# A fused retention and expert-attention kernel: another order of matmuls within a step

## The chip, the cores and the metric

One core of a Trainium2 chip runs the kernel. The metric is the device time of one execution in microseconds (us), which is the time of that one core. The kernel before was timed in three runs.

## The reference

Two layers stand one behind the other. The first is a retention layer without softmax: for 8 batches, 8 heads, 576 positions and a head dimension of 64, the scores are weighted with a power of gamma that depends on the distance, and masked causally.

```python
gamma = 1.0 - 2.0 ** (-5.0 - np.arange(H))
Dmat = np.where(rel >= 0, gamma[:, None, None] ** rel, 0.0)    # rel = i - j
attn = np.matmul(q @ k.T / 8 * Dmat, v)
x = attn.transpose(0, 2, 1, 3).reshape(B, S, H * D)            # 8 x 576 x 512
```

The second layer takes x, picks 2 of 4 experts for each position with a small gate, and runs a causal softmax attention with one head of 64 in each expert. The outputs of the two chosen experts are added with the weights of the gate.

```python
logits = x @ w_gate                  # top 2 of 4, softmax over these two: w
for e in range(4):
    q, k, v = x @ wq[e], x @ wk[e], x @ wv[e]
    a = softmax(causal(q @ k.T / 8))
    out += chosen(e) * w(e) * (a @ v @ wo[e])
```

All inputs and outputs are float32.

## The kernel before, in words

**Steps.** The retention is computed in the chunked form, with chunks of 64 positions and a running state per head. A step n takes 128 positions (two chunks) of two batches, so 36 steps (NC) cover everything; nine steps make one pair of batches. In the retention of a step there are four kinds of small float32 matmuls, all 64 by 64 on a quarter of the TensorE array:

- `qk(n)` (L115 to L132): the products of queries and keys inside a chunk. ScalarE copies them from PSUM to `p` (L127) and GpSimd masks them (L130).
- the *old* products in `result` (L155): state times query. ScalarE copies them to `x32` (L158).
- the *own* products in `result` (L168): values times the masked products of the same chunk. VectorE adds them to `x32` (L172 copies where there is no state yet, L173 adds).
- `state(n)` (L106): the new state's products `st`, which VectorE adds to the state (L111 copies for a first chunk, L113 adds).

`result(n)` is a generator; each `yield` is a place where the caller puts other work between. Its later parts scale `x32` with powers of gamma on GpSimd (L178) and split it into a high part `xh` (ScalarE, L181) and a low part `xl` (GpSimd, L183), so that the big projections can run as three float32r products each.

**The second layer's work.** `proj` (L213) makes keys or queries of two experts for 384 positions with twelve 128 by 384 matmuls (L226) in three groups of four, with a yield behind each group. `vproj` (L241) makes values and gate logits (L251). `outproj` (L431) is the last product (L440). `scores` and `score` (L322 to L380) do the softmax attention's scores of a tile of 128 positions: the first `next` issues all of the tile's score matmuls `ss` (L354, or L360 for the last, 64 wide tile of a batch), and the rest is the softmax, where VectorE masks, takes the row's extreme and moves the scores out of PSUM (L369, L373), and ScalarE does the exponential (L377). One step later `factors` (L382) and `scale` (L391) scale the rows, and `turn` (L398) transposes them by VectorE into the buffers `TA` and `TB` (L403, L405). When all of a batch's tiles are turned, `values` (L408) multiplies them with the values: 18 column blocks of the scores, for each 8 float32 matmuls (L418) into four PSUM tiles `ys`, which are accumulated over all blocks; then ScalarE and VectorE take them out as `yh` and `yl` (L424, L425).

**The order of the work.** Every engine is listed in `ORDERED`, so each engine executes its instructions in the order in which the program text issues them. The main loop (L677 on) does for each step n from 4 to 36: `factors` of the last step's tiles, `qk(n)`, the first part of `result(n-1)` (old, then own), `state(n)`, then, from step 7 (LAG) on, the score matmuls of this step's tiles, the scaling and the softmax, the loads for step n+2, the rest of `result`, and `work(n)`. A table, `STEPS`, written out by hand, says which projections, value products and output products step n does; `work(n)` issues them in the order keys and queries, values' projection, value products, output products, and between its pieces the loop issues transposes. In the steps with value products (12, 17, 22, 26, 31 and 35; `hold` in the code) the transposes come after all of `work`, because they would overwrite `TA` and `TB`. Behind the value products' place in `work` stands a count: before the change they are issued, all at once, when three groups of projections have been issued, which is after the keys and before the queries. Step 12 has only value products.

**PSUM.** All matmul results use one pool of eight banks (`pool`, `bufs=8`): `qk`, `old`, `own` and `st` take two banks each, a projection or an output product one, `ys` four. A step's scores take four banks, but two where the tile is one of the first two of a batch and stands alone (steps 7, 8, 16, 17, 25, 26, 34 and 35). A bank is given again in the order in which it is released, and TensorE waits in its queue when the tile that had the bank before has not been read out.

Of the kernel before, what the change touches and what calls it, by code (L numbers as in the profile page):

```python
# [27 lines left out]
LAG = 7  # L28


def f(ap):
    return ap.bitcast(F32)
# [3 lines left out]
def kernel(ctx: ExitStack, tc: tile.TileContext, xf, vkf, wraw,  # L36
# [14 lines left out]
    def bank(shape, name):  # L51
        return pool.tile(shape, F32, name=name, tag="b")
# [34 lines left out]
    def subs(n):  # L87
        return [divmod(2 * n + s, 9) for s in range(2)]
# [49 lines left out]
    def result(n):  # L138
        if n % 3 == 0:
            XR[n // 3] = [sa.tile([128, 4, NB], F32R, name="x" + y, bufs=2) for y in "hl"]  # L140
        xh, xl = XR[n // 3]
        l0 = n % 3 * 128
        old = [bank([128, 2, 128], "old") for g in range(2)]
        x, p, vk = X[n], P.pop(n), VK[n]
        x32 = sa.tile([128, 2, 2, 128], F32, name="x32", tag="x32", bufs=2)
        on, off = slice(0, 128), None
        for s, (b, k) in enumerate(subs(n)):
            i = slice(64 * s, 64 * s + 64)
            if k == 0:
                on, off = slice(64 - 64 * s, 128 - 64 * s), i  # L150
                continue
            for r in range(2):
                for g in range(2):
                    for u in range(2):
                        mm(old[g][HALF[u], r, i], S_[b, k - 1][HALF[g], r, u], x[HALF[g], 0, 2 * r + u, i],  # L155
                           start=True, stop=True)
        for g in range(2):
            act(x32[:, g, :, on], old[g][:, :, on], AF.Copy)  # L158
        if n == 4:
            build(4)  # L160
            gp.tensor_copy(gi[:, :, S:], gi[:, :, :64])
        own = [bank([128, 2, 128], "own") for r in range(2)]
        for s in range(2):
            i = slice(64 * s, 64 * s + 64)
            for g in range(2):
                for r in range(2):
                    for u in range(2):
                        mm(own[r][HALF[u], g, i], vk[HALF[r], s, 0, 2 * g + u], p[HALF[r], g, s, u],  # L168
                           start=True, stop=True)
        for r in range(2):  # L170
            if off:
                v.tensor_copy(x32[:, :, r, off], own[r][:, :, off])  # L172
            v.tensor_add(x32[:, :, r, on], x32[:, :, r, on], own[r][:, :, on])  # L173
        x32 = x32.rearrange("p g r i -> p (g r) i")
        yield
        e = gp if n > 2 else v
        t0 = 64 * subs(n)[0][1]
        e.tensor_mul(x32, x32, gi[:, :, t0:t0 + 128])  # L178
        if n > 4:
            decay(n + 2)  # L180
        act(xh[:, :, l0:l0 + 128], x32, AF.Copy)  # L181
        yield
        e.tensor_sub(xl[:, :, l0:l0 + 128], x32, f(xh[:, :, l0:l0 + 128]))  # L183
        yield
# [220 lines left out]
                v.transpose(TB[:, :nb - 8, z, k - 4], x[:, 8:])  # L405
            yield

    def values(b, s0, s1, cut=True):  # L408
        py = [bank([128, s1 - s0, 32], "ys") for g in range(4)]
        order = [j for m in range(s1) for j in (m, 2 * s1 - 1 - m)]  # L410
        for m, j in enumerate(order):
            sj = max(s0, j // 2)
            R, i = divmod(18 * b + j, 12)
            vq, jj = VQ[R], i % 4 * 3 + i // 4
            for z in range(2):
                tt = TA[:, j, z, sj:s1] if j < 8 else TB[:, j - 8, z, sj - 4:s1 - 4]
                for g in range(4):
                    mm(py[g][HALF[z], sj - s0:], vq[QUAD[g], jj, D * z:D * z + D], tt[QUAD[g]],  # L418
                       start=(m == 0), stop=(m == 2 * s1 - 1))
            if cut and m % 6 == 5 and m < 2 * s1 - 1:  # L420
                yield
        for g in range(4):
            hi, lo = (y[:, g // 2, 1 + s0:1 + s1, g % 2] for y in YS)
            act(hi, py[g], AF.Copy)  # L424
            v.tensor_sub(lo, py[g], f(hi))  # L425
        if b % 2 == 0:
            for y in YS:
                gp.tensor_copy(y[:, :, 0], f(y[:, :, 9]))
        yield
# [26 lines left out]
    STEPS = {}  # L456
    for P_ in range(NP):
        b, n = 2 * P_, 9 * P_
# [28 lines left out]

    def work(n):
        todo = STEPS.get(n, [])
        vals = [values(x[1], 0, 9, False) for x in todo if x[0] == "y"]  # L490
        bring = [x[1] for x in todo if x[0] == "back"]
        i = 0
        for kind, *w in todo:
            if kind == "kq":
                R, p, *m = w
                for m in m or "kq":
                    for _ in proj(R, m, p):
                        i += 1
                        for y in vals[:i == 3]:
                            next(y, None)  # L500
                        if i == 3 and bring:
                            back(bring.pop())
                        yield
            elif kind == "v":
                for _ in vproj(*w):
                    i += 1
                    if i == 3 and bring:
                        back(bring.pop())
                    yield
            elif kind == "o":  # L510
                for y in vals:
                    next(y, None)
                yield from outproj(w[0])
        for y in vals:
            for _ in y:
                yield
        for R in bring:
            back(R)

    def run(g):  # L520
        for _ in g:
            pass
# [114 lines left out]

    late = result(0)
    next(late)
    qk(1)  # L640
    fetch("k", nc.scalar)
    fetch("q", nc.scalar)
# [4 lines left out]

    late = result(1)
    next(late)
    qk(2)  # L650
    next(late)
    run(late)
    state(2)

    late = result(2)
    next(late)
    load(3, nc.scalar)
    weights("k", "h")
# [18 lines left out]
    for n in range(4, NC + 1):  # L677
        if n < LAG:
            load(n + 2)
        if n == 5:  # L680
            fetch("o")
        late = result(n - 1)
        now, old = TILES.get(n, []), TILES.get(n - 1, [])
        for x in old:
            factors(*x)
        if n < NC:
            qk(n)
        next(late)
        if n < NC:
            state(n)  # L690
        if n >= LAG:
            soft = scores(*now)
            next(soft)
            run(each(scale, old))
            run(soft)
            load(n + 2)
        gates(0)
        if n <= 5:
            decay(n + 1)
        run(late)  # L700
        for w in {4: "v", 7: "o"}.get(n, ""):
            weights(w)
        turns = each(turn, old)
        if n == 12:
            run(turns)
        hold = any(w[0] == "y" for w in STEPS.get(n, []))
        for _ in work(n):
            if not hold:
                next(turns, None)
        run(turns)  # L710
        if n < NC:
            gates(1)
# [53 lines left out]
```

## Time and profile before

| | us |
|---|---|
| median of three runs | 428.38 |
| lowest and highest | 424.47 and 432.3 |
| the profiled execution | 426.58 |
| its span, first to last instruction | 424.7 |
| TensorE matmul busy | 393.2 |
| VectorE busy | 265.3 |
| ScalarE busy | 283.4 |
| GpSimd busy | 167.3 |

The span is what the views below divide up; 1.9 us of the execution lie outside it. A float32 matmul of the program is two matmul and two weight-load instructions in the trace. Matmul ends are modelled, so that a short stall can hide inside time shown as busy; the starts are recorded. In the text a step is named by its number n; step 19 starts at 169.75 us, step 20 at 179.03, step 21 at 189.38, step 22 at 199.12, step 24 at 222.80, step 26 at 243.08, step 30 at 286.64 and step 31 at 295.59, each time being that of its first `qk` matmul.

### The profile page before, as it was taken

How to read it: one execution, taken by the hardware profiler on the slowest of the kernel's cores; microseconds unless marked ns; L12 is line 12 of the kernel's file. 1: busy time of each engine (PE TensorE's matmuls, PEld its weight loads, DVE VectorE, ACT ScalarE, POOL GpSimd, SP SyncE). 2: the span in 40 equal slices, each digit the busy share in tenths (PEclk: the TensorE clock that was granted, in tenths of full speed). 3: DMA queues.
4: the chain of work that ended last, by engine and by line, in shares of the span. 5: the costliest groups of instructions: out<-in, count | busy, mean ns of one | idle time of the engine just before them, and what ended most of it. 6: DMA issues, size and time to landing. Idle time of an engine off the chain costs nothing.

```text
span 424.7 us, 20358 instructions
## 1 busy us (share of the span) xinstructions
PE 393.2 (93%) x8742; PEld 333.8 (79%) x8742; DVE 265.3 (62%) x1103; ACT 283.4 (67%) x809; POOL 167.3 (39%) x182
## 2 busy tenths in 40 slices
PE   7597999996799999999998989999999999999894
PEld 3486898796688978897887978898788987887673
DVE  2745386765777726869296727677497726983931
ACT  4354469674597747878576747779587747797751
POOL 2217856443345534445354444444445432000000
PEclk9898999998999999999999999999999999999999
DMA  8568557464255536567264635566454221422331
GB/s 288 164 235 323 172 187 184 131 185 131 102 168 159 191 101 174 165 176 243 98 166 135 188 127 158 183 174 199 145 169 146 86 75 42 115 66 96 105 119 60
DMA packets 33689, 65.10 MB, mean 153 GB/s; under 512 B 3392, under 2 KB 19264, under 8 KB 33600
## 3 DMA queue, kind: packets, MB, share of 16 engines
q1 hardware_dynamic: 32304, 59.08, 44.4%
q10 hardware_dynamic: 1296, 4.72, 3.2%
q8 instruction: 69, 1.13, 1.2%
q14 instruction: 20, 0.16, 0.2%
HBM read 49.63 MB, written 14.16 MB: 150 GB/s over the span
## 4 chain that ended last, share of the span: by engine, by line
PE 83%; DVE 6%; issue 5%; DMA 3%; ACT 1%; SPq 1%; ACTq 1%; DVEq 0%
PE pj L226 25%; PE pv L251 13%; PE ys L418 12%; PE po L440 10%; PE ss L354 7%; PE qk L124 4%; PE own L168 4%; DMA vk<-vkf 3%; PE old L155 3%; PE st L106 3%; PE ss L360 2%; DVE yl L425 1%; DVE x L173 1%; DVE ta L403 1%; DVE p L369 1%
## 5 line engine op out<-in xcount | busy, mean ns | idle before, releaser
L377 ACT ACTIVATE p<-p,nm 128x64 f32<-128x64 f32 (+5 forms) x144 | 79.3, 552 | 18.0 <-DVE nm L369 13.4
L130 POOL TENSOR_SCALAR_AFFINE_SELECT p<-p 64x512 f32<-64x512 f32 x72 | 49.0, 680 | 95.4 <-ACT p L127 93.0
L395 ACT ACTIVATE p<-p,sm 128x64 f32<-128x64 f32 (+5 forms) x144 | 69.4, 567 | 9.5 <-DVE sm L389 5.6
L183 POOL TENSOR_TENSOR xl<-x,xh 128x512 fp32r<-128x512 f32 x33 | 42.4, 1284 | 60.5 <-ACT xh L181 60.5
L369 DVE CUSTOM_DVE_ANT_0 p<-ss,mask 128x128 f32<-128x128 f32 (+7 forms) x128 | 50.4, 452 | 4.4 <-PE ss L354 4.3
L173 DVE TENSOR_TENSOR x<-x,own 128x256 f32<-128x256 f32 (+1 forms) x72 | 25.5, 386 | 43.0 <-ACT x L158 35.7
L425 DVE TENSOR_TENSOR yl<-ys,yh 128x288 fp32r<-128x288 f32 (+2 forms) x36 | 12.8, 417 | 61.6 <-ACT yh L424 61.6
L178 POOL TENSOR_TENSOR x<-x,gi 128x512 f32<-128x512 f32 x33 | 42.5, 1289 | 18.2 <-DVE x L173 11.3
L403 DVE STREAM_TRANSPOSE ta<-p 128x256 f32<-128x256 f32 (+2 forms) x144 | 48.9, 367 | 0.2 <-ACT p L395 0.2
L418 PE MATMUL ys<-ta,vq 32*64 32x288 f32 (+6 forms) x1152 | 45.4, 365 | 3.8 <-issue 3.8
L418 PE MATMUL ys<-tb,vq 32*64 32x96 f32 (+4 forms) x1344 | 43.5, 248 | 5.0 <-issue 5.0
L418 PEld LDWEIGHTS ys<-tb,vq 32*64 32x64 f32 x1344 | 39.3, 134 | 7.2 <-issue 6.3
L418 PEld LDWEIGHTS ys<-ta,vq 32*64 32x64 f32 x1152 | 36.0, 133 | 8.4 <-issue 7.2
L354 PE MATMUL ss<-k,q 64*64 64x512 f32 (+7 forms) x512 | 38.5, 406 | 0.2 <-issue 0.2
L424 ACT ACTIVATE yh<-ys 128x288 fp32r<-128x288 f32 (+2 forms) x36 | 10.9, 389 | 38.1 <-PE ys L418 38.1
L448 ACT ACTIVATE ot<-po 128x512 f32<-128x512 f32 x35 | 19.9, 592 | 19.8 <-PE po L440 16.2
L95 POOL TENSOR_TENSOR vk<-vk,con 128x512 f32<-128x512 f32 x30 | 31.5, 1051 | 0.0
L127 ACT ACTIVATE p<-qk 128x256 f32<-128x256 f32 x72 | 23.7, 382 | 9.3 <-PE qk L124 8.3
L181 ACT ACTIVATE xh<-x 128x512 fp32r<-128x512 f32 x36 | 22.3, 618 | 10.5 <-POOL x L178 8.6
L106 PE MATMUL st<-vk 64*64 64x64 f32 x1024 | 24.1, 220 | 5.6 <-DVE vk L95 4.0
L113 DVE TENSOR_TENSOR s<-st,s 128x128 f32<-128x128 f32 x112 | 24.9, 281 | 6.2 <-PE st L106 6.2
L168 PE MATMUL own<-p,vk 64*64 64x64 f32 x1152 | 26.4, 222 | 2.0 <-issue 1.9
(86 smaller groups left out, 892.0 us busy)
## 6 DMA issues: line engine op xcount, KB each, us to landing
x<-xf SPq DMA_DIRECT2D x33, 512.0 KB, 4.5
vk<-vkf SPq DMA_DIRECT2D x33, 512.0 KB, 5.7
vq<-hv SPq DMA_DIRECT2D x48, 192.0 KB, 6.3
out<-ot SPq DMA_DIRECT2D x36, 256.0 KB, 2.3
hv<-vn SPq DMA_DIRECT2D x24, 192.0 KB, 2.6
ta<-wraw ACTq DMA_DIRECT2D x3, 512.0 KB, 5.6
x<-xf ACTq DMA_DIRECT2D x3, 512.0 KB, 4.3
vk<-vkf ACTq DMA_DIRECT2D x3, 512.0 KB, 6.2
```

Of the source, the lines that this page charges most:

```text
L130: gp.affine_select(w, w, pattern=[[0, 8], [1, 64]], base=0, channel_multiplier=-1, compare_op=OP.is_ge, fill=0.0)
L168: mm(own[r][HALF[u], g, i], vk[HALF[r], s, 0, 2 * g + u], p[HALF[r], g, s, u], start=True, stop=True)
L178: e.tensor_mul(x32, x32, gi[:, :, t0:t0 + 128])
L226: mm(ps, ww[:, kc, p * 128:(p + 1) * 128], xx[:, kc], start=(i == 0), stop=(i == 11))
L251: mm(ps, xx[:, kc, l0:l0 + 128], ww[:, kc], start=(i == 0), stop=(i == 11))
L354: mm(ps[u][HALF[p]], q(p, z, i), k[p][HALF[z], :ws[u]], start=True, stop=True)
L369: v.tensor_tensor_reduce(x, ps[u], mask[:, 512 - ws[u]:], -1.0, BIG, OP.add, OP.min, nm[:, u:u + 1])
L377: act(x, x, AF.Exp, bias=bias, scale=-1.0, accum_out=sm[:, 0, u:u + 1])
L395: act(x, x, AF.Copy, scale=sm[:, 1, u:u + 1])
L403: v.transpose(TA[:, :min(nb, 8), z, k], x[:, :min(nb, 8)])
L418: mm(py[g][HALF[z], sj - s0:], vq[QUAD[g], jj, D * z:D * z + D], tt[QUAD[g]], start=(m == 0), stop=(m == 2 * s1 - 1))
L440: mm(ps, yy[:, p], ww[:, p], start=(i == 0), stop=(i == 5))
```

## The change

Two things are moved; no instruction is added or taken out.

In the steps without value products, the score matmuls of step n are issued between the old and the own products. In the steps with value products they stay behind `state(n)`. For that, `result` has one more yield, between old and own, and the three calls ahead of the loop that want both parts call `next` twice.

In the steps with value products, `values` is cut in two halves of nine column blocks. The first half is issued first in `work(n)`, ahead of the projection of the keys; the second half when four groups of projections have been issued, which is after the keys and the first third of the queries. The tail's calls of `values` keep their cut of six blocks.

```diff
@@ result
             gp.tensor_copy(gi[:, :, S:], gi[:, :, :64])
+        yield
         own = [bank([128, 2, 128], "own") for r in range(2)]
@@ values
-    def values(b, s0, s1, cut=True):
+    def values(b, s0, s1, part=6):
...
-            if cut and m % 6 == 5 and m < 2 * s1 - 1:
+            if m % part == part - 1 and m < 2 * s1 - 1:
                 yield
@@ work
-        vals = [values(x[1], 0, 9, False) for x in todo if x[0] == "y"]
+        vals = [values(x[1], 0, 9, 9) for x in todo if x[0] == "y"]
...
+        for y in vals:
+            next(y)
...
-                        for y in vals[:i == 3]:
+                        for y in vals[:i == 4]:
                             next(y, None)
@@ the main loop
         next(late)
+        hold = any(w[0] == "y" for w in STEPS.get(n, []))
+        if n >= LAG:
+            soft = scores(*now)
+        if n >= LAG and not hold:
+            next(soft)
+        next(late)
         if n < NC:
             state(n)
         if n >= LAG:
-            soft = scores(*now)
-            next(soft)
+            if hold:
+                next(soft)
             run(each(scale, old))
             run(soft)
             load(n + 2)
```

The line that computed `hold` further down is gone. VectorE's and ScalarE's own orders in a step without value products stay as they were: adds of own, adds of the state, softmax.

More of the change, by code (lines that the diff above doesn't have):

```diff
@@ L649 @@
     next(late)
+    next(late)
     qk(2)
@@ L655 @@
     late = result(2)
+    next(late)
     next(late)
@@ L688 @@
         next(late)
+        hold = any(w[0] == "y" for w in STEPS.get(n, []))
[3 more added lines that the diff above has]
+            next(soft)
+        next(late)
         if n < NC:
@@ L705 @@
             run(turns)
-        hold = any(w[0] == "y" for w in STEPS.get(n, []))
         for _ in work(n):
```

## The prediction

> **What bounds the kernel now.** I read the page first, then the waits, then the timelines of single steps.
>
> ```profile
> span 424.7 us, 20358 instructions
> PE 393.2 (93%) x8742; PEld 333.8 (79%) x8742; DVE 265.3 (62%) x1103; ACT 283.4 (67%) x809; POOL 167.3 (39%) x182
> PE 83%; DVE 6%; issue 5%; DMA 3%; ACT 1%; SPq 1%; ACTq 1%; DVEq 0%
> q8 instruction: 69, 1.13, 1.2%
> ```
>
> TensorE is busy for 93% of the span, and the chain that ended last is TensorE for 83%. A busy share is no proof, so next come the waits of TensorE alone, in the stretch from 60 to 350 us, which is nearly all of the main loop:
>
> ```profile
> PE ys L418 <- issue: 7.0, 5, 3.8
> PE pj L226 <- DVE x L173: 2.0, 2, 1.4
> PE st L106 <- issue: 1.5, 1, 1.5
> PE ss L360 <- issue: 1.1, 1, 1.1
> PE old L155 <- issue: 1.0, 1, 1.0
> ```
>
> That is all but 0.2: 12.8 us of 290. Every other phase follows the one before without a gap. So whatever the order of the matmuls, the change can give back at most these 12.8 us, and of them 3.8 stand ahead of the value products of step 12, which wait for transposes and keep their place, and 1.4 in step 13 come from VectorE. About 7.5 us are within reach. On the other side nothing protects TensorE: each new wait of it is paid in full. The question is therefore which new waits the new order makes.
>
> **How a projection waits for VectorE.** Step 31 shows it.
>
> ```profile
> 297.28 1.40 PE L354 MATMUL ss<-k,q 64*64 64x320 f32 x15
> 298.76 0.16 DVE L389 TENSOR_TENSOR sm<-sm,wt 128x4 f32<-128x4 f32 x1
> 298.87 0.75 DVE L173 TENSOR_TENSOR x<-x,own 128x256 f32<-128x256 f32 x2
> 299.54 0.48 DVE L111 COPY s<-st 128x128 f32<-128x128 f32 x2
> 299.34 0.97 PE L226 MATMUL pj<-xh,whk 128*128 128x384 f32 x4 [0.66 <-DVE x L173]
> ```
>
> A step with four score banks uses eight banks for qk, old and the scores, and four for own and st; the first tile of `work` gets the bank that is released next, the first of own. VectorE was late here (L389 is the last step's factors), its add began at 298.87, and the projection started 0.47 after that start. In all but two steps this wait is hidden, because the state products and the scores run on TensorE while VectorE adds:
>
> ```profile
> 170.50 0.66 PE L168 MATMUL own<-p,vk 64*64 64x64 f32 x32
> 170.97 0.66 PE L106 MATMUL st<-vk 64*64 64x64 f32 x32
> 171.25 0.29 DVE L172 COPY x<-own 128x128 f32<-128x128 f32 x1 [3.65 <-PE own L168]
> 171.43 1.81 PE L354 MATMUL ss<-k,q 64*64 64x448 f32 x16
> 171.51 0.29 DVE L173 TENSOR_TENSOR x<-x,own 128x128 f32<-128x128 f32 x1
> 173.17 0.62 PE L226 MATMUL pj<-xh,whk 128*128 128x384 f32 x2
> ```
>
> In step 19 VectorE begins on own 0.28 after st begins; the first bank is free at about 171.80, and the projection starts at 173.17. The cover is the scores.
>
> **Part 1, the scores between old and own.** Now own and st are last, so only st's 0.46 (170.97 to 171.43) is left as cover. VectorE begins 0.28 after st begins, as the row shows, and the projection can start 0.47 later (step 31): 0.28 + 0.47 - 0.46 = 0.3 us of new wait. In steps 10, 14, 19, 23, 28 and 32 a batch begins and VectorE does a copy and an add for the first bank (171.25 to 171.80, 0.55, and 0.1 for the release): 0.28 + 0.65 - 0.46 = 0.47. Steps 7, 8, 16, 25, 34 have two score banks and use old's banks next, 36 has no st and qk: nothing. Step 13 waits for a late VectorE already. That leaves, without 21 and 30 (below), nine steps at 0.3 and six at 0.47: 2.7 + 2.8 = 5.5 us. In two of them (10 and 24) a stall of another kind falls behind own and hides 0.8: **+4.7**. Bounds: 0, if the adds are done within st's time, and 0.9 a step (VectorE's whole add and release, 0.75 + 0.1), 13 us.
>
> What else moves with it: own and st are some 1.2 to 1.7 us later. VectorE already stood idle ahead of own; it waits for ScalarE's copy of old as it is:
>
> ```profile
> DVE x L173 <- ACT x L158: 35.7, 18, 4.0
> vk<-vkf SPq DMA_DIRECT2D x33, 512.0 KB, 5.7
> ```
>
> Its chain through the step starts up to 1.75 later (step 19: 173.17 - 0.46 + 0.28 = 172.99, against 171.25). The load of `vk` waits in SyncE's queue for own, with hv, vq and out behind it, so all go out 1.2 to 1.7 later; vk lands 5.7 after its issue and is wanted by GpSimd a step (9 us) later, so this costs nothing here. If that cover were gone it would cost up to the 1.7 in a step.
>
> **Part 2, values first.** Four `ys` banks are wanted at once where one projection bank was. In steps 17, 26 and 35 (two score banks) they are old's two and own's two:
>
> ```profile
> 244.77 0.97 PE L354 MATMUL ss<-k,q 64*64 64x192 f32 x15
> 245.11 0.76 DVE L173 TENSOR_TENSOR x<-x,own 128x256 f32<-128x256 f32 x2 [1.48 <-ACT x L158]
> 245.67 0.96 PE L226 MATMUL pj<-xh,whk 128*128 128x384 f32 x4
> ```
>
> Both adds end at 245.87 and the fourth bank is free at 245.96, where TensorE wants it at 245.67: 0.3 each, and 0.3 more in step 17, whose VectorE comes later: **+1.2**. In steps 22 and 31 they are own's two and st's two, so L111 too must be done, and VectorE is late from the step before:
>
> ```profile
> 191.41 0.75 DVE L173 TENSOR_TENSOR x<-x,own 128x256 f32<-128x256 f32 x2 [3.48 <-ACT x L158]
> 201.17 0.74 DVE L173 TENSOR_TENSOR x<-x,own 128x256 f32<-128x256 f32 x2
> 201.83 0.48 DVE L111 COPY s<-st 128x128 f32<-128x128 f32 x2
> 202.15 0.97 PE L226 MATMUL pj<-xh,whk 128*128 128x384 f32 x4
> 288.67 0.75 DVE L173 TENSOR_TENSOR x<-x,own 128x256 f32<-128x256 f32 x2 [3.48 <-ACT x L158]
> 289.80 0.72 PE L440 MATMUL po<-who,yh 128*128 128x512 f32 x2
> ```
>
> Between the adds at 191.41 and at 201.17 VectorE has no rest, as between 288.67 and 298.87. In step 30 st would begin 0.46 ahead of the output products at 289.80 and the add 0.28 behind that, at 289.62: 0.95 later than now, and with it all that follows. In step 31 the add comes at 299.8; the last state copy ends 1.15 behind that (298.87 to 300.02 above) and frees its bank in 0.1, so values start at 301.05, where the projection started at 299.34: **+1.7** for steps 30 and 31 together. Steps 21 and 22 are built alike: the add at 202.1, values at 203.3 for 202.15: **+1.1**. Bounds for the two pairs: 0 and 4. Moved without a price: the evacuations of `ys` end 0.8 later against the step's end, because a third of the queries' projection now stands ahead of the second half; steps 18, 23, 27 and 32 want own's adds 1.2 later as well, which covers it.
>
> **Part 3, the stalls marked issue.** They stand inside unbroken runs of matmuls, with no releaser. From the chain, steps 24, 17 and 26, and last the busy times of the values' instructions in step 17 (TensorE's matmuls, then its loads):
>
> ```profile
> 222.87 0.62 PE qk L124 x32
> ...
> 225.39 1.07 issue
> 226.46 1.19 PE ss L360 x12
> ```
> ```profile
> 156.39 0.93 issue
> ```
> ```profile
> 253.32 1.21 issue
> ```
> ```profile
> 147.00:160.60 13.60, 6.15 (x288) 5.40 (x288) 1.55 (x4) 1.32 (x4) 1.00 0.30 101
> ```
>
> The instruction queue moved 69 packets for 17,484 TensorE instructions, about 253 each. In step 24 the four small phases are 256 instructions in 2 us, and the stall follows; the values' 576 take 6.15 us, 94 an us; four projection matmuls with their four loads take up to 0.97, some nine an us. So I read these stalls as the next block of instructions not being there: from 222.87 to 226.46, 3.6 us, for one block. By that reading a block that takes longer than 3.6 us costs nothing. With scores of 1.1 us in the middle step 24's block takes 3, so most of its 1.07 goes, and the part hidden behind modelled ends too: -1.1. The 1.5 in step 10 comes amid heavy DMA and I leave it. A half of the values is 288 instructions in 3.1 us and is followed by sixteen slow projection matmuls, so a block seldom lies inside: of the values' 7.0 - 3.8 = 3.2 in five steps I take two thirds, -2.1. Together **-3.2**; bounds 0 and -5.8 (3.2 + 1.1 + 1.5).
>
> [...]
>
> **The sum.** 4.7 + 1.2 + 1.7 + 1.1 - 3.2 = +5.5 us on the profiled execution's 426.58 (span 424.7 and 1.9 around it): 432.1. That execution lies 1.8 under the median of the runs shown, 428.38; on the median the forecast is **433.9 us**, 1.3% more. A measurement of this kernel can tell about 2%, 8.6 us, from no change.
>
> **The rivals.**
>
> *Relief without the waits* (the other side: faster than before). Nothing of parts 1 and 2 is paid, because the tile behind own gets a bank that is free already, or VectorE is done within st's 0.46. It decides where the add starts no later than st. Then part 3 alone is left: 428.4 - 3.2 = 425.2, at its bound 422.6. For it: only two projections in the loop wait on L173 now. Against it: eight banks are taken when own begins, and the rows for 0.28 and 0.47.
>
> *VectorE becomes the bound.*
>
> ```profile
> 180.28 0.16 DVE L389 TENSOR_TENSOR sm<-sm,wt 128x4 f32<-128x4 f32 x1
> ```
>
> Its chain from own's add to the next factors' end is 9.2 us in step 19 (171.25 to 180.44), without rest, in a step of 9.28; a start 1.75 later leaves it no slack, and a lateness of 0.5 beyond the 0.3 in each of 17 steps gives 8.5 more: 442. Against it: it is busy for 62% of the span, so other steps let it catch up.
>
> *Relief is nothing.* The blocks are fetched as slowly as before, because a later `vk` load keeps the DMA queues full when they are asked for, and a stall appears elsewhere. Then 428.4 + 8.7 = 437.1. For it: the 1.5 of step 10, amid loads. [...]
>
> **How the numbers follow.** The forecast 0.50, with its own range 429 to 438; relief without waits 0.18; relief nothing 0.20; VectorE the bound 0.12. To leave out no more than 2 in 10 the range goes from 424 (most of the first rival) to 440 (between the last two). Faster by over 2% needs 419.8, below the bound of the first rival, and is left with 0.04. Slower by over 2% (437) takes most of the last rival, half of the third and a tenth of the forecast: 0.10 + 0.10 + 0.05 = 0.25. Within 2%: 0.71.
>
> **What would show it.** Right: waits of the first projection, value or output matmul on DVE x L173 (its line moves by one) in some 15 steps, 0.3 to 0.5 each, and of values on the state's adds in steps 22 and 31, over 1 us; VectorE's idle time ahead of own released by TensorE's own and no longer by ScalarE; stalls marked issue inside values down to one or two. Wrong: if projections still start straight behind st in steps 14, 15, 18 to 20, part 1 has failed; if values have their stalls as before, part 3; if VectorE's adds begin over 0.5 after own's end in most steps, the second rival is at work.

## The result: 1.5% longer, and where the time went

The kernel after takes 434.0 us (median of six runs, 430.79 to 437.18). In the same runs the kernel before takes 427.01 us (424.47 to 432.3). The ratio is 1.0146, with a 95% interval from 1.0103 to 1.0188: slower, by less than 2%. The profiled execution of after took 430.79 us, the fastest of the six, and that of before 426.58; what follows is read from these two.

These lines of its page answer to those of before: the span, the engines, the chain, and VectorE's additions of the own products (their line is L174 now).

```profile
span 429.1 us, 20334 instructions
PE 394.7 (92%) x8742; PEld 338.3 (79%) x8742; DVE 267.0 (62%) x1103; ACT 282.5 (66%) x809; POOL 167.8 (39%) x182
PE 69%; DVE 18%; issue 4%; DMA 3%; ACT 3%; POOL 1%; SPq 1%; ACTq 0%; DVEq 0%
L174 DVE TENSOR_TENSOR x<-x,own 128x256 f32<-128x256 f32 (+1 forms) x72 | 25.5, 386 | 41.1 <-PE own L169 16.7
```

No engine executes more instructions than before, and the busy times are nearly the same. What changed is the chain that ended last: VectorE holds 18% of it instead of 6%. The largest part of VectorE's idle time ahead of its additions is now ended by TensorE's own products (16.7 of 41.1 us); before it was ScalarE's copy of old (35.7 of 43.0). TensorE's waits in the main loop, from 60 to 355 us (us in total, times, longest), show the exchange:

```profile
PE pj L227 <- DVE x L174: 6.1, 10, 1.7
PE ys L419 <- issue: 4.6, 2, 3.8
PE ys L419 <- DVE x L174: 1.8, 2, 0.9
PE pj L227 <- issue: 0.9, 1, 0.9
PE ss L355 <- ACT k L236: 0.4, 1, 0.4
PE old L155 <- issue: 0.3, 1, 0.3
PE st L106 <- issue: 0.2, 1, 0.2
```

Before there were 2.0 us of waits on VectorE and 10.8 us of stalls marked issue; now there are 7.9 and 6.0, and 0.4 of a wait on ScalarE. So waits came and stalls went, but the view shows only 1.5 us of loss, because parts of both lie behind matmul ends that are modelled. The starts of the steps are recorded and measure better. Length of a step after, minus before, in us:

```
batch begins      14 +0.29   19 +0.27   28 +0.29   32 +0.29   23 +0.64
other steps       15 +0.34   18 +0.14   27 -0.12   30 +0.17   33 +0.17    9 +0.54
behind a gate     11 +0.82   20 +0.79   29 +0.79
value products    17 +0.24   22 +0.91   26 +0.01   31 +1.06   12 +0.89
a stall gone      10 -1.49   24 -1.57   13 -0.47   21 -0.27
two score banks   16 -0.10   25 -0.05   34 -0.05
```

Steps 10 to 34 are 4.0 us longer together. Inside them the stalls marked issue, taken as distances between recorded starts (the list in experiments 9 and 10), sum to 8.75 us before and to 3.26 after, without step 12's wait for transposes. So 5.5 us of stalls went and 9.5 us of other time is new. Both are rough, because such a distance holds the usual spacing of the starts as well: in experiment 9, with the order of before, step 17 has a stall of 0.52 and is 0.74 us shorter than before, where experiment 4 has none there and is 0.76 shorter.

Three rows of the table need a word. In step 9 the scores, which come earlier now, wait 0.4 us for ScalarE's copy of the keys (the row L355 <- ACT k L236). In step 15 a stall of 0.27 us and in step 27 of before one of 0.24, both too small for the list, fall at such a place; without them these two steps would be like 18, 30 and 33. And the 0.89 of step 12 is a matter of TensorE's clock (see below).

**An ordinary step.** Step 19 after, which begins at 170.91 us (timeline of TensorE and VectorE):

```profile
171.66 1.79 PE L355 MATMUL ss<-k,q 64*64 64x448 f32 x16
173.27 0.64 PE L169 MATMUL own<-p,vk 64*64 64x64 f32 x32
173.73 0.65 PE L106 MATMUL st<-vk 64*64 64x64 f32 x32
174.02 0.29 DVE L173 COPY x<-own 128x128 f32<-128x128 f32 x1 [4.50 <-PE own L169]
174.22 0.28 DVE L174 TENSOR_TENSOR x<-x,own 128x128 f32<-128x128 f32 x1
174.65 0.42 PE L227 MATMUL pj<-xh,whk 128*128 128x384 f32 x1 [0.27 <-DVE x L174]
```

VectorE begins 0.29 behind the start of st, and the projection starts 0.63 behind that: the prediction has 0.28 and 0.65. The projection is 0.27 later than without a wait, not 0.47, and the step is 0.27 longer.

**A step behind a gate.** In steps 10, 19 and 28 VectorE also computes a gate (L294 to L315) and ends it in the next step, which loses 0.8. Step 20 after:

```profile
181.85 1.46 DVE L315 TENSOR_TENSOR wt<-ex,mx 64x6 f32<-64x6 f32 x4
182.42 0.64 PE L169 MATMUL own<-p,vk 64*64 64x64 f32 x32
182.88 0.65 PE L106 MATMUL st<-vk 64*64 64x64 f32 x32
183.74 0.16 DVE L390 TENSOR_TENSOR sm<-sm,wt 128x4 f32<-128x4 f32 x1
183.85 0.75 DVE L174 TENSOR_TENSOR x<-x,own 128x256 f32<-128x256 f32 x2
184.32 0.97 PE L227 MATMUL pj<-xh,whk 128*128 128x384 f32 x4 [0.79 <-DVE x L174]
```

Before, the four small products of L314 took 0.69 and GpSimd's select came afterwards:

```profile
179.16 0.69 DVE L314 TENSOR_TENSOR wt<-ex,mx 64x6 f32<-64x6 f32 x4
180.49 1.37 POOL L130 TENSOR_SCALAR_AFFINE_SELECT p<-p 64x512 f32<-64x512 f32 x2 [2.01 <-ACT p L127]
```

Before, these products began 0.13 us into step 20; now 1.39 us into it (it begins at 180.46), because VectorE's whole chain starts later. There they meet the select and take 1.46, and VectorE comes to the own products 0.97 behind the start of st, not 0.28. In steps 22 and 31 the same products, which VectorE now comes to 1.15 and 0.66 us later in the step, meet one select and take 1.16 us instead of 0.68. Step 22:

```profile
202.33 1.16 DVE L315 TENSOR_TENSOR wt<-ex,mx 64x6 f32<-64x6 f32 x4
```

### The profile page after: what moved, and what is told of

Same layout as the page of the kernel before. It is cut to its first block, busy times and chain, and to the rows that moved or that the text cites. A ratio compares the mean times of both kernels' runs of the same rounds, so it can differ in the third digit from the quotient of the medians.

```text
span 429.1 us, 20334 instructions
## 1 busy us (share of the span) xinstructions
PE 394.7 (92%) x8742; PEld 338.3 (79%) x8742; DVE 267.0 (62%) x1103; ACT 282.5 (66%) x809; POOL 167.8 (39%) x182
## 3 DMA queue, kind: packets, MB, share of 16 engines
q8 instruction: 69, 1.13, 1.1%
## 4 chain that ended last, share of the span: by engine, by line
PE 69%; DVE 18%; issue 4%; DMA 3%; ACT 3%; POOL 1%; SPq 1%; ACTq 0%; DVEq 0%
PE pj L227 19%; PE ys L419 13%; PE pv L252 12%; PE po L441 9%; PE ss L355 5%; PE qk L124 4%; DMA vk<-vkf 3%; PE own L169 3%; DVE p L370 3%; DVE x L174 2%; PE old L155 2%; DVE wt L315 2%; DVE ta L404 2%; DVE s L113 1%; PE st L106 1%
## 5 line engine op out<-in xcount | busy, mean ns | idle before, releaser
L419 PE MATMUL ys<-ta,vq 32*64 32x256 f32 (+6 forms) x1152 | 48.5, 373 | 6.4 <-issue 4.6
L174 DVE TENSOR_TENSOR x<-x,own 128x256 f32<-128x256 f32 (+1 forms) x72 | 25.5, 386 | 41.1 <-PE own L169 16.7
L419 PEld LDWEIGHTS ys<-ta,vq 32*64 32x64 f32 x1152 | 37.2, 136 | 13.0 <-issue 6.9
L355 PE MATMUL ss<-k,q 64*64 64x64 f32 (+7 forms) x512 | 37.6, 406 | 0.4 <-ACT k L236 0.4
L169 PEld LDWEIGHTS own<-p,vk 64*64 64x64 f32 x1152 | 24.4, 137 | 8.2 <-issue 5.6
L227 PE MATMUL pj<-xh,whk 128*128 128x384 f32 x96 | 23.3, 363 | 8.0 <-DVE x L174 6.1
L124 PEld LDWEIGHTS qk<-x 64*64 64x64 f32 x1152 | 20.9, 137 | 9.1 <-issue 5.3
```

Of the source, the lines that this page charges most:

```text
L227: mm(ps, ww[:, kc, p * 128:(p + 1) * 128], xx[:, kc], start=(i == 0), stop=(i == 11))
L355: mm(ps[u][HALF[p]], q(p, z, i), k[p][HALF[z], :ws[u]], start=True, stop=True)
```

## The experiments

The theory: the loss is the cover that part 1 took from VectorE's additions, and the gain is that TensorE outruns its instruction blocks less often. The rivals: the values in their new place cost the time; or where the blocks happen to end decides. Ratios are against the kernel before, timed beside each experiment on the same chip; experiments 1 to 4 ran on one chip, 5 to 11 on another.

**1. The scores alone** (part 1 without part 2).

```diff
-        vals = [values(x[1], 0, 9, 9) for x in todo if x[0] == "y"]
+        vals = [values(x[1], 0, 9, 18) for x in todo if x[0] == "y"]
...
-        for y in vals:
-            next(y)
...
-                        for y in vals[:i == 4]:
+                        for y in vals[:i == 3]:
```

> Part 1 alone: the scores stand between old and own in the steps without value products; the value products stay whole behind the keys. Theory (own's bank is handed to the first tile of work, and its read-out by VectorE lost its cover): TensorE waits on L174 before the first projection, value or output matmul in some 15 steps, 0.15 to 0.3 us each and 0.8 in steps 11, 20 and 29, where VectorE is late; the fetch stalls of steps 7, 10, 21 and 24 shrink by 3 to 4 us together. Net 0 to +3 us, ratio 1.000 to 1.007. Rival (VectorE becomes the bound): +6 us or more. Rival (the loss is all in the value products' part): 3 to 4 us faster.

Measured: 433.75 us, ratio 1.0158 [1.0109, 1.0206]. The whole loss is here: more than the 1.007 expected, and near the 6 us of the first rival. Steps 11, 20, 29 (+0.81), 14 (+0.28), 19 (+0.27), 23 (+0.65) are as in the kernel after, and so are steps 22 and 31 at the place where work begins: the projection starts 4.05 and 4.33 us into the step, where in the kernel after the values start at 4.03 and 4.31.

**2. The values alone** (part 2 without part 1: the changes to `values` and `work` on the kernel before).

> Part 2 alone: the value products first, in halves round the keys' projection; the scores stay behind the state products. Theory: values wait for own's and the state's banks, 0.3 us in steps 17, 26 and 35, 0.4 in step 22 and some 1.4 in step 31 (0.7 of which the projection waits there already); the halving takes 1 to 2 us of fetch stalls away. Net 0 to +2 us, ratio 1.000 to 1.005, and no projection waits on L173 but in step 13. Rival (the value products' place carries the whole loss): +4 us or more. Rival (the loss is all in the scores' place): 2 us faster.

Measured: 431.18 us, ratio 1.0068 [1.0033, 1.0102]. Slower by itself, and over the 1.005 expected. The halves give no relief when the first stands behind the small matmuls: TensorE's stalls inside the values, worked out as in experiment 9, sum to 4.7 us in the main loop against 4.45 before, 1.93 of it in step 26. Not all that this profile lost is the halves' doing: step 10 has a stall of 2.8 us, against 1.7 before, and behind the stall in step 26 TensorE's granted clock is 0.50 for 3.41 us.

**3. Own ahead of the scores, st behind them** (old, own, scores, st).

```diff
         next(late)
+        hold = any(w[0] == "y" for w in STEPS.get(n, []))
+        if n >= LAG:
+            soft = scores(*now)
+        if n >= LAG and not hold:
+            next(soft)
         if n < NC:
             state(n)
         if n >= LAG:
-            soft = scores(*now)
-            next(soft)
+            if hold:
+                next(soft)
...
```

> In the steps without value products the order is old, own, scores, state: the scores still break the burst of small matmuls, but they stand behind own and cover VectorE's adds again; values as before. Theory (cover): no wait on own's adds in steps 9 to 11, 14, 15, 18 to 20, 23 to 30, 32, 33; fetch stalls of 7, 10, 21 and 24 as small as in the changed kernel; 3 to 5 us faster than before, ratio 0.988 to 0.994. Rival (any split of the small matmuls costs, by turns between kinds of matmul or by the later state products): at or above the time of scores between old and own.

Measured: 430.68 us, ratio 1.0061 [1.0025, 1.0096]: a miss. The cover theory is right for the ordinary steps, which stay within 0.04 us of before (14, 18, 19, 23, 28, 30, 32, 33). But steps 11, 20, 29, 22 and 31 lose 0.69, 0.79, 0.79, 1.19 and 0.62 all the same. VectorE works in the order issued, and its additions to the state now wait for st behind the scores. Step 19:

```profile
172.37 0.66 PE L106 MATMUL st<-vk 64*64 64x64 f32 x32
172.96 0.97 PE L226 MATMUL pj<-xh,whk 128*128 128x384 f32 x4
173.05 0.88 DVE L113 TENSOR_TENSOR s<-st,s 128x128 f32<-128x128 f32 x4 [1.06 <-PE st L106]
```

So VectorE is late here too, and its gate products meet the select again: they take 1.04, 1.55 and 1.54 us in steps 11, 20 and 29, and 1.15 and 1.16 in 22 and 31. Step 20:

```profile
180.10 1.55 DVE L314 TENSOR_TENSOR wt<-ex,mx 64x6 f32<-64x6 f32 x4
```

So a late VectorE is a cost of its own, beside the lost cover. The rows of step 19 also give a number that the prediction lacked: with own's additions done before st begins (they end at 171.98), the projection still starts 0.59 behind st's start, not 0.46.

**4. The values' halves behind the keys** (before, with the first half where the whole stood, and the second a third of the queries later; no part 1).

```diff
-        vals = [values(x[1], 0, 9, False) for x in todo if x[0] == "y"]
+        vals = [values(x[1], 0, 9, 9) for x in todo if x[0] == "y"]
...
-                        for y in vals[:i == 3]:
+                        for y in vals[:i in (3, 4)]:
...
```

> The value products in halves, but the first half behind the keys' projection, where they stood whole; the second half behind the first third of the queries; scores as before. Theory (instruction blocks): the stalls marked issue inside the values of steps 17, 22, 26 and 35, 3.2 us in the profile of before, shrink to 1 or less, with no new wait on VectorE: 1.5 to 2.5 us faster, ratio 0.994 to 0.997. Rival (the stalls have to do with DMA traffic and not with the run of short matmuls): they stay or move, ratio 0.999 to 1.001.

Measured: 426.28 us, ratio 0.9952 [0.9918, 0.9986], faster than both kernels. Behind slow projections the halves stall less: the sum of stalls inside the values goes from 4.45 to 1.28.

**5 and 6. VectorE later by a known amount.** Two extra reads of own's first bank, whose result nothing uses, ahead of VectorE's additions, in the kernel after and in the kernel before.

```diff
...
+        if n >= 8:
+            for g in range(2):
+                v.tensor_copy(scr, own[0][:, g])
```

> The changed kernel with two more VectorE copies of half of own's first bank ahead of own's adds from step 9 on, some 0.45 us that nothing uses: the suspected wait made longer. Theory (TensorE waits for own's first bank): each wait grows by 0.4 to 0.5 in the 17 steps with four score banks and in the steps with value products, some 8 us more than the changed kernel, ratio to before about 1.033. Rival (VectorE has time to spare and the loss comes from the order on TensorE): no more than 1 us more, ratio 1.015.

> The kernel before with the same two copies. Theory: the scores behind own cover 0.5 us or more, so the steps without value products don't move; steps 13 and 31, and a few steps in which VectorE is late as it is, pay: 1 to 2 us, ratio 1.002 to 1.005. Rival (0.45 us of VectorE costs the same in either order): the same addition as in the changed kernel.

Measured: after, 446.54 us, ratio 1.0478 [1.0398, 1.0559], where the kernel after has 1.0146; its profiled span is 14.0 us longer (443.1 against 429.1); before, 432.01 us, ratio 1.0131 [1.005, 1.0212]. More than expected in both. The steps tell them apart. In the kernel after, the step grows by 0.46 (14), 0.49 (18), 0.45 (19), 0.48 (33): all of the 0.43 to 0.47 by which the additions begin later in the step. In the kernel before, the same steps change by 0.02 at most. TensorE's waits, first with the reads after, then before:

```profile
PE pj L231 <- DVE x L178: 10.6, 10, 2.1
PE pv L256 <- DVE x L178: 4.0, 6, 0.7
PE ys L423 <- DVE x L178: 3.9, 3, 1.5
```

```profile
PE st L107 <- issue: 4.2, 2, 3.4
PE pj L230 <- DVE x L177: 2.8, 2, 1.5
```

What the kernel before loses in its profile stands in step 10 (3.5 us, the stall of 3.4 above), in step 7 (2.5) and in step 31 (0.9), one of the two that were expected to pay; step 13, the other, paid 0.1. In steps 7 and 10 TensorE's granted clock is 0.50 for 3.41 us each, which the profile of before does not have there. How much of its 1.3% the reads cause, and not such stalls and clocks, stays open. The kernel after with the reads has one such stretch too, in step 13, which grows by 2.4. In the kernel after there is no slack left between own and the next product, which is the theory's main claim.

**7 and 8. GpSimd's select later.** From step 8 on, the select of `p` is issued in the rest of `result`, behind GpSimd's scaling there, instead of at once; on the kernel after, and on experiment 4.

```diff
             act(p[:, g], ps[g], AF.Copy)
+        if n < 8:
+            select(n)
+
+    def select(n):
+        if n >= NC:
+            return
...
             decay(n + 2)
+        if n >= 7:
+            select(n + 1)
         act(xh[:, :, l0:l0 + 128], x32, AF.Copy)
```

> The changed kernel with GpSimd's masking of the products (the select on L130) issued behind the decay of the values, 3 to 4 us later in the step, instead of straight behind ScalarE's copies. Theory (VectorE's later chain now meets the select, and its small operations stand still till the select ends): the last gate operations take 0.7 again instead of 1.2 to 1.5, the waits of 0.8 in steps 11, 20 and 29 fall to 0.15, those of steps 22, 23 and 31 by 0.5: 3 to 4 us less than the changed kernel, ratio to before 1.006. Rival (VectorE is late by its own amount of work): the long operations stay, ratio 1.014.

> The order of before with the values in halves, the first behind the keys' projection, and with GpSimd's select late as in the run before this. Theory: in the old order VectorE met the select only in steps 13 and 31, so the select gives 0.5 to 1 us on top of the 0.5% of the halves: ratio 0.992 to 0.995. Rival (the select's later end holds up own in the next step): slower than the halves alone, ratio 0.998 or more, with TensorE waiting for GpSimd ahead of own.

Measured: 432.01 us, ratio 1.0119 [1.0068, 1.017], for the kernel after; 427.09 us, 0.9995 [0.9952, 1.0038], for experiment 4. The first moved less than expected, and the timing alone can't tell it from the kernel after; its trace does. The second stands where the rival had it (0.998 or more), but its trace shows no wait of TensorE for GpSimd ahead of own, and its interval overlaps that of experiment 4. So the late select was worth nothing that the timing shows in the old order, and the 0.5% of the halves was not found a second time.

In the trace of the first, the small products of step 20 are back at 0.68, and the wait falls:

```profile
183.66 0.68 DVE L323 TENSOR_TENSOR wt<-ex,mx 64x6 f32<-64x6 f32 x4
184.88 0.75 DVE L180 TENSOR_TENSOR x<-x,own 128x256 f32<-128x256 f32 x2
185.35 0.97 PE L235 MATMUL pj<-xh,whk 128*128 128x384 f32 x4 [0.42 <-DVE x L180]
```

Steps 11, 20 and 29 lose 0.45, 0.42 and 0.43 now. The rest of the 0.77 by which the products had grown (1.46 against 0.69) went to other operations, which the moved select now meets: L304's pair takes 0.72 from start to next start where it took 0.36. A new stall of 1.34 marked issue in step 15 took back what was won.

How long the four products `wt<-ex,mx` take goes with the selects beside them. In the kernels before and after they take 0.68 to 0.69 us together where no select begins ahead of the last of them, 0.98 where the first waits for the end of one, 1.16 to 1.17 beside a whole one or parts of two, and 1.46 to 1.47 beside two; in step 20 after they end at 183.31, 0.01 us behind the end of the second select. The additions of own, with one operand in PSUM, were not slowed: in the kernel before, 29 of them run within a select, in 0.27 to 0.29 (128 wide) and 0.41 to 0.42 us (256 wide), as without one. Why the products are slowed and these additions not, no run shows.

**9 and 10. 128 more TensorE instructions at the start** (the qk products of step 0 three times, about 1 us, same result), on the kernels before and after.

```diff
-                        mm(ps[g][HALF[r], s, u], x[HALF[g], 1, h, i], x[HALF[g], 0, h, i], start=True, stop=True)
+                        for again in range(3 if n == 0 else 1):
+                            mm(ps[g][HALF[r], s, u], x[HALF[g], 1, h, i], x[HALF[g], 0, h, i],
+                               start=True, stop=True)
```

> The kernel before with the qk matmuls of step 0 issued three times over (the same result is written again): 128 more TensorE instructions at the start, about 1 us, and nothing else. If the stalls marked issue are blocks of 256 instructions that are not there yet, they stand again at every 256th instruction of the trace, which is now 128 instructions earlier in the program. By the trace of before, the blocks that TensorE would then run through in under 2.7 us end in the values of steps 17 (2.46 us), 22 (2.66 and 2.29), 26 (2.41) and 31 (2.52), in the scores of steps 18 (1.88) and 25 (1.86). So the stalls of steps 10 and 24 go and new ones come in 18 and 25; the time is 0.997 to 1.006. Rival: the stalls belong to their places (small phases, loads in flight): 10 and 24 keep theirs of 1.5, 18 and 25 have none, and the time is 1.002.

> The kernel after with the same 128 more TensorE instructions in step 0. If the waits on VectorE are the loss, the steps 11, 14, 15, 18 to 20, 28 to 30, 32 and 33 stay as long as in the kernel after, within 0.05 us where no stall marked issue falls into them, and the time is 1.011 to 1.019. The blocks run through fastest then end in the state products of steps 18 (2.77 us by the trace of after) and 25 (1.93) and in the values of step 22 (2.14), so stalls of 0.5 to 1.5 come there. Rival: a good part of the loss is where the blocks happen to end; then the ratio falls below 1.008 or rises over 1.022.

Measured: before, 427.71 us, ratio 1.0001 [0.996, 1.0042]; after, 430.85 us, 1.01 [1.0059, 1.0141]. Counting TensorE's matmuls, loads and semaphore instructions in time order, every stall marked issue of over 0.45 us from step 10 to 35 falls on the same count modulo 256, except step 12's wait for transposes, and 1.2 to 1.6 us behind the end of a packet of the instruction queue (step, us of the stall, count modulo 256):

```
before              10 1.72  13 1.26  17 1.25  21 0.57  22 1.01  24 1.47  26 1.47  35 0.72     all 193
before, 128 more    12 0.98  13 1.15  17 0.52  18 0.53  22 0.76  28 0.89  30 1.88  31 0.78
                    34 0.64  35 0.51                                                           all 193
after               13 0.52  17 1.04  21 0.47  26 1.23                                         all 193
after, 128 more     12 0.87  17 0.93  26 0.55                                                  all 193
```

The stalls moved to other places of the program, and the count stayed. Those of steps 10 and 24 are gone from the kernel before (-1.78 and -1.73) with nothing changed there. Of the places named, step 18 and the values of 17 and 22 came; step 25 and the values of 26 and 31 did not, and 12, 28, 30 and 34 came unnamed (13 and 35 have one in both kernels, and that of 31 stands at a projection): a block run through fast makes a stall likely, no more. In the kernel after, the steps with waits on VectorE stay as they were to 0.02 us (11 +0.82, 14 +0.30, 19 +0.27, 20 +0.79, 23 +0.66, 29 +0.80, 33 +0.16). The ratio, 1.01, lies just under the 1.011 that was expected, and its interval reaches below the rival's 1.008; it is the steps that tell. By them the waits on VectorE are not an accident of where the blocks end.

**11. Scores in the middle, values behind the keys** (experiments 1 and 4 together).

```diff
-        for y in vals:
-            next(y)
...
-                        for y in vals[:i == 4]:
+                        for y in vals[:i in (3, 4)]:
```

> The kernel after with the two halves of the values one place later: the first half when three groups of projections are issued, the second when four are. So part 1 as it is, and the values behind the keys. If the two parts add up, the time is that of the scores in the middle alone (1.0158) and of the halves behind the keys alone (0.9952) together: 1.008 to 1.013; steps 17 and 26 lose their stall inside the values, and steps 22 and 31, whose values then wait for no bank, come to +0.6 each as with the scores alone, instead of +0.9 and +1.06. Rival: values first are worth something beside the scores in the middle; then it is no faster than the kernel after, 1.0146 or more.

Measured: 429.91 us, ratio 1.0052 [1.0006, 1.0098], better than expected. That it is faster than the kernel after rests on two chips (1.0146 there); against the kernel after with 128 more instructions, on the same chip, the medians are 0.9 us apart and the intervals overlap. TensorE's waits in the loop:

```profile
PE pj L227 <- DVE x L174: 7.3, 12, 1.1
PE ys L419 <- issue: 3.8, 1, 3.8
PE old L155 <- issue: 0.9, 1, 0.9
```

The waits on VectorE are those of the scores alone; of the values' stalls only the 3.8 of step 12 is left. Against the kernel after, steps 17 and 26 are 1.0 and 0.9 us shorter, and 22 and 31 0.47 each; the profiled executions as a whole do not show it (432.56 and 430.79), because this one is longer outside steps 10 to 34. By these four steps the price of values first is not a new wait at their beginning, but stalls inside a half that follows the small matmuls, and in 22 and 31 two banks that the state's additions hold. In step 22 after:

```profile
204.63 0.76 DVE L174 TENSOR_TENSOR x<-x,own 128x256 f32<-128x256 f32 x2
205.11 1.21 PE L419 MATMUL ys<-ta,vq 32*64 32x288 f32 x10 [0.90 <-DVE x L174]
205.30 0.48 DVE L111 COPY s<-st 128x128 f32<-128x128 f32 x2
205.94 0.40 PE L419 MATMUL ys<-ta,vq 32*64 32x288 f32 x1
```

## Why the prediction was right, and which of its terms were not

The forecast of 433.9 us stood against 434.0, and +5.5 on the profiled execution against +4.2. The direction and the mechanism held: lost cover in nearly every step, against relief from instruction blocks. Several terms were off and made up for each other, and the nearness of the two numbers is luck: between the medians timed together the change is 7.0 us, between the profiled executions 4.2, and 0.9 of these 4.2 stand in step 12, for which the prediction has no term.

**Part 1.** The two durations of the wait, 0.28 and 0.65, were measured as predicted. But the ordinary steps pay 0.14 to 0.17 instead of 0.3, and those where a batch begins 0.27 to 0.29 instead of 0.47. The step that failed is the cover of "st's 0.46": that is the distance from st to the scores, and the first product of `work` follows st only after 0.59 to 0.67 in experiment 3 and 0.58 with two score banks. With 0.6 for 0.46 the prediction's own sums give 0.15 and 0.33. The kernel before paid the same behind the scores: 1.74 from scores to projection in step 19, where scores to own take 1.61 after.

Steps 11, 20 and 29 were put with the ordinary ones at 0.3 and lost 0.8 each; this is the second rival at work in three steps, with a cause that it didn't name. Experiment 7, the late select on the kernel after, takes back about half of it, so the select is shown for that half, and the other half went to other operations that the moved select meets. Its chain of 9.2 us without rest was the right row; what the later start ran into was GpSimd's select. Step 23 lost 0.64, and 0.65 or 0.66 in experiments 1, 7, 10 and 11: VectorE begins 0.64 behind st there, out of idle time, and not 0.29; why stays open. Without 10 and 24 the 13 steps of part 1 lost 5.25 us where 4.75 was predicted: the ordinary ones cost half, and three cost more than twice as much.

**What moves with it.** The later `vk` load cost nothing that the trace shows; GpSimd's own lateness, through its select, is what the prediction did not follow.

**Part 2.** +1.2 in steps 17, 26 and 35 for the fourth bank: the wait does not exist. In steps 17, 26 and 35 of the kernel after the values start 0.91 behind the scores, as the projection did. Steps 30 and 31 lost 1.23 together (1.7 predicted); 21 and 22 lost 0.64, net of the 1.0 us stall that left step 22 (1.1 predicted). But experiment 1 loses 0.6 in 22 and 31 with the values in their old place: VectorE's lateness from part 1 makes most of this, 0.48 of it the gate products beside a select, and the state's banks make the other 0.47 (experiment 11).

**Part 3.** Relief of 3.2 was predicted; by the distances between starts 5.5 was seen in steps 10 to 34. The reading of the stalls held in experiments 9 and 10: they stand at the count 193 modulo 256, 1.2 to 1.6 us behind the end of a packet. Two sizes were wrong. Step 10's 1.5 was left, with heavy DMA as the reason (a share of 0.69 from 73.3 to 75.3 us), and went. Of the five kernels with the scores behind st and with nearly this count of instructions (before and experiments 2, 4, 6 and 8) all five have that stall, 1.7 to 3.6 us; of the five with the scores in the middle (after and experiments 1, 5, 7 and 11) none. In step 24 it is four of five, and none of five. So the scores in the middle give the block its time in both steps, as the prediction had it for step 24 alone. It isn't the only way: 128 instructions more remove both stalls as well, and in experiment 4 step 24 has none.

The values' -2.1 was not the halves' doing by themselves: experiment 2 has 4.7 us of stalls in the values. (The five steps that the prediction named hold four such stalls before, in 17, 22, 26 and 35.) Less than that came where both parts stand together (1.04 in the kernel after, and 1.23 at the projection behind a half) or where the halves follow projections (1.28 in experiment 4). The prediction's argument, that a half is followed by slow projection matmuls, forgot what stands ahead of it: four small phases and the scores, which are fast too.

Most blocks end without a stall: in steps 10 to 35 some fifty packets of the instruction queue end (49 before, 48 after), and 3 to 10 stalls stand there in each kernel. These last 0.5 to 3.6 us, so the rival in which relief is nothing did not come.

**Step 12** grew by 0.89 with its order unchanged. Three windows of it, before and then after: TensorE idle, and the two halves of its value products (us of the window, busy us of PE, PEld, DVE, ACT and POOL with counts, granted TensorE clock, DMA share, GB/s):

```profile
96.80:100.50 3.70, 0.00 (x0) 0.00 (x0) 3.60 (x26) 3.24 (x16) 1.93 (x2) 1.00 0.79 271
100.50:104.50 4.00, 3.96 (x100) 3.99 (x105) 1.05 (x3) 0.78 (x4) 1.27 (x1) 0.57 0.04 15
104.50:108.30 3.80, 3.80 (x206) 3.52 (x190) 0.00 (x0) 0.00 (x0) 0.00 (x0) 1.00 0.02 4
```

```profile
96.55:100.30 3.75, 0.00 (x1) 0.00 (x0) 3.65 (x26) 3.26 (x17) 2.00 (x2) 0.91 0.76 282
100.30:104.70 4.40, 4.35 (x109) 4.33 (x113) 1.06 (x3) 0.79 (x4) 1.26 (x1) 0.50 0.03 7
104.70:109.00 4.30, 4.30 (x194) 4.08 (x182) 0.00 (x0) 0.07 (x1) 0.00 (x0) 0.79 0.01 4
```

TensorE stands idle in the first row of each; behind it the mean granted clock falls to 0.57 and to 0.50, and is 0.79 in the last row after. The trace's clock records tell why. The clock is granted by half in one stretch, which is twice as long after:

```profile
100.92:104.33 3.41, 3.41 (x91) 3.41 (x95) 0.63 (x2) 0.36 (x1) 1.27 (x1) 0.50 0.03 8
```

```profile
99.64:106.47 6.83, 6.12 (x160) 6.10 (x168) 1.69 (x6) 1.45 (x6) 1.26 (x1) 0.50 0.03 11
```

In all 13 traces this stretch lasts either 3.41 or 6.83 us. It is the short one where it begins 3.8 us or more behind the end of step 12's last score matmul (before and experiments 1, 2, 4, 6, 8, 9 and 10), and the long one where it begins 2.1 to 3.6 us behind it (after and experiments 3, 5, 7 and 11). So the 0.89 is the second 3.41 us at half clock. Experiment 10 is the kernel after but for 128 instructions at the start and has the short stretch, and so has experiment 1: the scores in the middle do not settle it. As all six traces with the scores behind st have the short stretch, and four of the six with the scores in the middle the long one, an influence is not excluded either. Nor does the half clock begin at a fixed distance from the last matmul: in four kernels (after and experiments 3, 5 and 11) it is 2.1 to 3.1 us behind its modelled end, in the kernel before 4.13. What sets its beginning and its length, no run shows. The prediction has no such term.

**The rivals.** Relief without waits fell: in experiment 5 all of an added lateness reaches TensorE. Relief is nothing fell with the count of stalls. VectorE as the bound is true in part: in steps 11, 20 and 29, and in 22 and 31, not in seventeen.

## What to carry to other kernels

Work that stands between an engine's product and the product that reuses its bank is cover, even if it looks like ordinary work (here the scores behind own: without them the ordinary steps paid 0.14 to 0.17 us, and those where a batch begins 0.27 to 0.29): before moving it, add up the reader's start, its duration and the release against what is left between. Use as what is left the distance that the trace shows for that very pair of neighbours, not that of another pair. Where TensorE runs through many tiny matmuls, put slow ones on both sides of them; here halves behind projections gained 0.5% (experiment 4; 0.05%, no more than noise, beside the late select in experiment 8), and the same halves behind other small matmuls lost 0.7%. Ask also what a later start of a side engine runs into: here VectorE's small products ran into GpSimd's select and took 1.46 us for 0.69.

## What the runs showed of the hardware that was not expected

- A stall marked issue can fall at a fixed count of TensorE's instructions: 193 modulo 256 in the two kernels and in both with 128 more, 0.5 to 1.9 us there, and for every stall of over 1 us without a releaser from step 10 to 35 in the other nine, in the first four kernels 1.2 to 1.6 us behind the end of a 16 KB packet of the instruction queue (69 packets and 1.13 MB in each of the kernels before and after). With 128 more instructions ahead the stalls moved to other places of the program, and the time stayed (1.0001).
- Four VectorE products of 64 by 6 elements took 0.68 to 0.69 us where no GpSimd select began ahead of the last of them, and 1.46 to 1.47 beside two.
- After 3.2 to 4.5 us without a matmul in step 12, TensorE's granted clock was 0.50 for 3.41 or for 6.83 us, never for anything between; where it was 6.83 in the kernel after, step 12 was 0.89 us longer.
- A projection follows 64 by 64 products 0.58 to 0.67 us behind the start of the last of these phases, where another small phase follows after 0.46.
